# Six token groups of a linear-attention and mixer kernel, run as three pairs with seven products for eight in both channel layers

## Chip, cores and metric

One core of a Trainium2 chip. The time is that of the device, in microseconds (us), for one launch. The engines are TensorE (PE, with its weight loads as PEld), VectorE (DVE), ScalarE (ACT), GpSimd (POOL) and SyncE (SP, which here only issues DMA transfers). Transfers are issued from SP's queue and from ACT's.

## What is computed

```python
# q, k, v: batch 8, heads 8, seq 576, head_dim 64
q_s = softmax(q, axis=-1); k_s = softmax(k, axis=2)
kv = np.einsum('bhsd,bhse->bhde', k_s, v)
attn = np.einsum('bhsd,bhde->bhse', q_s, kv)
x = attn.transpose(0, 2, 1, 3).reshape(8, 576, 512)
h = np.maximum(x.transpose(0, 2, 1) @ w_tok1, 0) @ w_tok2      # 576 -> 256 -> 576
u = x + h.transpose(0, 2, 1)
out = u + np.maximum(u @ w_ch1, 0) @ w_ch2                     # 512 -> 1536 -> 512
```

## The kernel before

A product in full precision is made of three matmuls: each operand is split into a high part (ACT, a cast) and a low part (DVE, the difference), and high x high, low x high and high x low are added up in PSUM. `split` does this; its two lines, L134 and L135, serve all operands.

**Units.** A unit is one batch and two heads (32 in all, four a batch). `load_unit` loads k twice (`kt_t` and `k_t`) and q on SP's queue, `softmax_k` and `softmax_q` run on DVE, ACT and POOL, `stage_qT` turns q on DVE and through DRAM (a store `q<-cv_s` and four loads `q_t<-q`), `stage_kv`, `stage_y`, `stage_h1` and the two halves of `stage_u` run on PE. The result, u, is split and kept in one of three slots of SBUF (`slots`, `uT`), each for one group.

**Groups.** The 8 x 576 tokens are nine groups of 512. For a group, `ch1` makes a 128-row block f of the hidden layer (12 blocks), `ch2` adds its share into four PSUM banks, `out_end` adds u and stores. The list `steps` puts groups 0 and 1 first, while weights are still loaded, then group 2, and so on. `n0` is the step at which group 2 begins; `put(at, ...)` hangs the stages of the units on these steps.

**Seven products for eight.** Two by two blocks of a matrix product can be had with seven block products (P1 to P7) in place of eight, if sums of weight blocks and sums of data blocks are formed first. `keep_blocks` and `keep_sums` form the weights of ch1 and store them in DRAM (`scratch_w`), `keep_out` and `keep_out_sums` those of ch2 (`scratch_v`). From there each product's weights, 256 KB, are loaded into a ring of buffers (`ring`, L588), eight ahead, each load behind the product that used the buffer before.

Groups 3 to 6 use this for ch1 alone, each group by itself, with its two halves of 256 tokens as columns (`data_sums`, `product` at L645, `pair_a`, `pair_b`); ch2 stays at eight products for eight (`ch2`, L694). Groups 7 and 8, called GA and GB, run as a pair in `both_groups`: the two groups are the column blocks, so that a product has 512 columns, and both ch1 and ch2 take seven products (`six`, L768 and L882). Hidden blocks are put together on DVE and ACT from seven results, in banks that are handed out in turn (`bank`).

The order on each engine is made when the kernel is built, by a scheduler that goes by the order of the code and by its own estimate of times; it moves instructions past each other where nothing forbids it.

## Time and profile before

| | |
|---|---|
| median of 3 runs | 795.43 us (793.12 to 795.67) |
| profiled execution | 796.62 us, span 794.8 us, mean granted clock 0.998 |
| PE, DVE, ACT, POOL busy | 97%, 78%, 43%, 23% of the span |
| matmuls | 4824 |
| moved by DMA | 174.83 MB, mean 220 GB/s |
| groups 3 to 6 | about 331 to 670 us |
| groups 7 and 8 as a pair | about 670 us to the end |

The span runs from the first to the last instruction on the core. Busy time of an engine is the union of its instructions' durations; that of PE includes the drain of each matmul, so that a PE busy all the time may still be fed slowly. The DMA share is the mean busy share of the 16 DMA engines and can pass 1 in a short window.

### The profile page before, as it was taken

To read this page: it belongs to the slowest core of one execution; us is meant where nothing else is said; L and a number is where in the kernel's file an instruction comes from. 1 tells how busy PE (TensorE), PEld (TensorE's weight loads), DVE (VectorE), ACT (ScalarE), POOL (GpSimd) and SP (SyncE) were. 2 spreads that over 40 slices of the span, in tenths; PEclk is the share of its full clock that TensorE was granted. 3 is DMA by queue.
4 is the path that set the end of the run, shared out by engine and by line. 5 is a ranking of instruction groups with operands and counts; after the bars stand their busy time and mean duration, and the time that the engine had idled before them with its cause. 6 is when DMAs were issued, how large, how long until landed. Compare 5 with 4: busy or idle time off the path is not lost.

```text
span 794.8 us, 13455 instructions
## 1 busy us (share of the span) xinstructions
PE 769.0 (97%) x4824; PEld 670.9 (84%) x4824; DVE 618.1 (78%) x1101; ACT 341.9 (43%) x744; POOL 180.7 (23%) x130
## 2 busy tenths in 40 slices
PE   3899999999999999999999999999999999999998
PEld 2688888877888888899999999989999998888886
DVE  7979998978788874878688657888987557667971
ACT  4666433444454443434353334434444324346610
POOL 0000000011111352122211111232422320536640
PEclk9999999999999999999999999999999999999999
DMA  9655644158879785587879777999978543667776
GB/s 304 187 174 166 224 150 171 44 171 278 273 243 336 232 286 177 144 282 210 238 213 287 226 219 216 288 339 314 316 233 270 161 134 115 195 189 198 192 207 196
DMA packets 151459, 174.83 MB, mean 220 GB/s; under 512 B 51297, under 2 KB 98017, under 8 KB 151393
## 3 DMA queue, kind: packets, MB, share of 16 engines
q1 hardware_dynamic: 145056, 161.65, 67.2%
q10 hardware_dynamic: 6336, 12.32, 4.1%
q8 instruction: 38, 0.62, 0.3%
q14 instruction: 29, 0.23, 0.1%
HBM read 131.47 MB, written 42.47 MB: 219 GB/s over the span
## 4 chain that ended last, share of the span: by engine, by line
PE 70%; DVE 11%; issue 7%; DMA 7%; ACT 2%; POOL 1%; SPq 1%; DVEq 0%; POOLq 0%; ACTq 0%
PE ps_o L694 20%; PE ps_h L645 14%; PE ps_h L768 7%; PE ps_o L768 7%; PE ps_h L464 6%; PE ps_h L422 4%; PE ps_h L487 4%; PE ps_h L357 2%; DMA q_t<-in_q 2%; DMA stg<-whole 1%; PE ps_h L430 1%; PE ps_o L464 1%; PE ps_o L882 1%; DMA w<-stg 1%; DVE q_t L340 1%
## 5 line engine op out<-in xcount | busy, mean ns | idle before, releaser
L694 PE MATMUL ps_o<-h,c2h 128*128 128x512 f32 x544 | 184.2, 398 | 2.9 <-ACT h L490 1.9
L694 PEld LDWEIGHTS ps_o<-h,c2h 128*128 128x128 f32 x544 | 101.4, 188 | 23.8 <-ACT h L490 3.0
L694 PE MATMUL ps_o<-h,c2l 128*128 128x512 f32 x272 | 106.0, 393 | 0.0
L318 POOL TENSOR_TENSOR k_t<-k_t,dg 128x640 f32<-128x640 f32 x24 | 41.6, 1735 | 217.6 <-ACT dg L317 182.1
L135 POOL TENSOR_TENSOR ql<-q_t,qh 128x640 fp32r<-128x640 f32 x24 | 38.4, 1599 | 182.3 <-PE ps_o L694 104.2
L645 PE MATMUL ps_h<-th,ring 128*128 128x256 f32 x384 | 72.3, 283 | 0.0
L645 PEld LDWEIGHTS ps_h<-th,ring 128*128 128x128 f32 x384 | 60.1, 191 | 0.0
L694 PEld LDWEIGHTS ps_o<-h,c2l 128*128 128x128 f32 x272 | 51.3, 188 | 8.6
L487 PE MATMUL ps_h<-uh,c1l 128*128 128x512 f32 x144 | 56.2, 390 | 0.0
L487 PE MATMUL ps_h<-ul,c1h 128*128 128x512 f32 x144 | 56.2, 390 | 0.0
L487 PE MATMUL ps_h<-uh,c1h 128*128 128x512 f32 x144 | 56.1, 392 | 0.0
L645 PE MATMUL ps_h<-uh,ring 128*128 128x256 f32 x288 | 54.4, 282 | 0.6 <-DVE c L672 0.6
L645 PE MATMUL ps_h<-tl,ring 128*128 128x256 f32 x192 | 54.3, 283 | 0.0
L645 PEld LDWEIGHTS ps_h<-uh,ring 128*128 128x128 f32 x288 | 46.5, 190 | 2.8 <-DVE c L672 0.8
L471 ACT CAST uh<-ps_h 128x320 fp32r<-128x320 f32 (+4 forms) x76 | 24.4, 334 | 52.1 <-PE ps_h L464 32.1
L336 ACT ACTIVATE q_t<-q_t 128x640 f32<-128x640 f32 x32 | 23.6, 738 | 46.1 <-DVE q_t L327 43.1
L326 DVE TENSOR_REDUCE st<-q_t 128x10 f32<-128x640 f32 x32 | 26.1, 815 | 22.2 <-DMA q_t<-in_q 22.2
L490 ACT ACTIVATE h<-ps_h 128x512 fp32r<-128x512 f32 x36 | 21.5, 598 | 49.5 <-PE ps_h L487 42.0
L645 PE MATMUL ps_h<-ul,ring 128*128 128x256 f32 x144 | 40.6, 282 | 0.0
L645 PEld LDWEIGHTS ps_h<-tl,ring 128*128 128x128 f32 x192 | 36.8, 192 | 0.0
L472 DVE TENSOR_TENSOR ul<-ps_h,uh 128x320 fp32r<-128x320 f32 (+4 forms) x76 | 27.4, 370 | 9.0 <-ACT uh L471 8.8
L135 DVE TENSOR_TENSOR qtl<-q_t,qth 128x512 fp32r<-128x512 f32 (+1 forms) x48 | 25.6, 566 | 8.1 <-ACT qth L134 7.3
(319 smaller groups left out, 2070.2 us busy)
## 6 DMA issues: line engine op xcount, KB each, us to landing
ring<-w SPq DMA_DIRECT2D x210, 256.0 KB, 3.7
ring<-v SPq DMA_DIRECT2D x42, 256.0 KB, 3.0
kt_t<-in_kt SPq DMA_DIRECT2D x32, 320.0 KB, 3.7
q_t<-in_q SPq DMA_DIRECT2D x32, 320.0 KB, 3.7
v_t<-in_v SPq DMA_DIRECT2D x32, 320.0 KB, 4.5
stg_w<-in_w SPq DMA_DIRECT2D x18, 512.0 KB, 6.0
k_t<-in_k SPq DMA_DIRECT2D x24, 320.0 KB, 4.9
q<-cv_s SPq DMA_DIRECT2D x24, 320.0 KB, 3.2
```

Of the source, the lines that this page charges most:

```text
L135: lo_eng.tensor_tensor(lo, src, f32(hi), op=ALU.subtract)
L318: nc.gpsimd.tensor_tensor(kx, kx, dg.unsqueeze(1).broadcast_to([P, C1, P]), op=ALU.subtract)
L326: nc.vector.tensor_reduce(st[:, 0, :], qt, axis=AX.X, op=ALU.max)
L336: nc.scalar.activation(qc, qc, AF.Exp)
L422: nc.tensor.matmul(y[:, 0:TOK], a, w, start=(i == 0), stop=(i == len(mm) - 1))
L464: nc.tensor.matmul(t[:, 0:N], a, w, start=(i == 0), stop=(i == len(mm) - 1))
L471: nc.scalar.copy(uh, src).ins,
L472: nc.vector.tensor_tensor(ul, src, f32(uh), op=ALU.subtract).ins,
L487: nc.tensor.matmul(t, a[:, n, :], w, start=(i == 0), stop=(i == 3 * NJ - 1))
L645: nc.tensor.matmul(t[:, cols], a, b[:, n], start=(i == 0), stop=(i == 5))
L694: m = nc.tensor.matmul(o, a[:, cs], w, start=(first and i == 0), stop=(last and i == 2))
L768: nc.tensor.matmul(o, a, b, start=first and i == 0 and (n == 0 or not one), stop=last and i == 2 and (n == 1 or not one))
```

## The change

Groups 3 to 8 become three pairs (`NR` = 3), each run by `both_groups(r, laters[r])`, with ch1 and ch2 at seven products for eight and 512 columns throughout. `data_sums`, `product`, `pair_a`, `pair_b` and `wide_*` go.

- ch1 of a pair works in six fixed PSUM banks (`places`), and units have two others (`pu`). Products are chained in a bank: P1 is written, copied by ACT; P6 is added to it and copied; P7 is added and copied; P4 is added, and the result goes through the Relu. P5 and P3 share a second bank, P2 has a third. So the sums that DVE formed of single results are now in part sums that PE accumulates.
- The pieces of u of groups 5 to 8 are no longer split at once. `stage_u` copies them (ACT) and stores them to DRAM (`u_kept`); `make_first`, `make_second` and `make_third` load them during ch2 of the pair before, form the sums and split them. The rows to be added at the end are loaded again (`residuals`).
- Units move forward: batches 3 and 4 run beside group 2 (eight units, four before), batches 5 and 6 beside the first pair, batch 7 beside the second (`SPACE`); none is left for the third.
- The sums of the c2 weights (`keep_out_sums`) take the weights from DRAM, where `load_pair` and `load_ch` now store them (`whole_out`, ACT's queue), instead of adding high and low part on POOL; all six run beside the first pair (`SUMS_AT`).
- The weights ring has eight buffers for all of 3 x 84 products, and each product issues the load for the eighth after it.

```diff
-    KEEP = (5.5, 7.5, 37, 38.5, 40, 41.5)
-    AHEAD = 12
+    AHEAD = 9
+    SUMS_AT = (4, 9, 14, 19, 24, 29)
+    RES_AT = 31
+    SPACE = ((5, 7, 1, 8), (7, 8, 1, 10), (8, 8, 0, 0))
...
+        t = load_weights(AT_C2 + f)
+        split(*c2_row(f), t, nc.vector)
...
+        nc.scalar.dma_start(whole_out[f // 2][:, f % 2 * CW : (f % 2 + 1) * CW], t.bitcast(F32))
...
-    uT = [slots[i] for i in (0, 1, 2, 1, 0, 2, 1, 0, 2)]
+    uT = [slots[i] for i in (0, 1, 2, 1, 0)]
...
+                if g >= len(uT):
...
+                    nc.scalar.copy(x[:, k1 - k0 : k1 - k0 + a1 - a0], t[:, a0 - n0 : a1 - n0])
+                    u["kept"][g][1] = k1 + a1 - a0
+                    if a1 == S or (g == b and a1 == edge):
+                        nc.scalar.dma_start(u_kept[g][j, :, k0 : k1 + a1 - a0], x[:, 0 : k1 - k0 + a1 - a0])
+                    continue
...
-        nc.gpsimd.tensor_tensor(a, f32(wh[:, i : i + 2]), f32(wl[:, i : i + 2]), op=ALU.add)
+        nc.sync.dma_start(f32(hi), whole_out[p])
...
+    TURN = (P1, P5, P6, P2, P7, P3, P4)
+    items = [("a", 0, e) for e in TURN[:5]]
+    for p in range(1, NP):
+        items += [("a", p, P1), ("a", p, P5), ("a", p - 1, P4), ("a", p - 1, P3), ("a", p, P6), ("a", p, P2), ("a", p, P7)]
+    tail = [("b", c, e) for e in TURN for c in range(NP)]
+    items += tail[:2] + [("a", NP - 1, P4), ("a", NP - 1, P3)] + tail[2:]
...
+        for k in range(2):
+            b11, b12, b21, b22 = (h_of[2 + i][:, 1] if k else row_place() for i in range(4))
+            for t, (i, n) in ((b11, (0, k)), (b12, (1, k)), (b22, (1, 2 + k)), (b21, (0, 2 + k))):
+                nc.sync.dma_start(t, u_kept[g + i][n])
+            t0, t1 = sum_place(), sum_place()
+            split(*of_first[k], b11, nc.vector)
+            vec(t0, b12, b11, op=sub)
+            split(*of_T[0][k], t0, nc.vector)
...
+            x, y = sets[(p + r) % 2]
+            z = places[4 + p % 2]
+            o = {P1: x, P6: x, P7: x, P4: x, P5: y, P3: y, P2: z}[e]
...
+            six(w, *zip(*src), [o], e in (P1, P5, P2), e in (P4, P3, P2))
...
+            if e == P1:
+                nc.scalar.copy(c11, o)
+            elif e == P6:
+                nc.scalar.copy(c12, o)
+            elif e == P2:
+                vec(c11, o, c11, op=add)
+                relu(c11)
+            elif e == P7:
+                nc.scalar.copy(c21, o)
+                vec(c22, y, c21, op=add)
+                relu(c22)
+            elif e == P4:
+                nc.scalar.activation(c21, o, AF.Relu)
+            elif e == P3:
+                vec(c12, o, c12, op=add)
+                relu(c12)
...
+        for i, (kind, p, e) in enumerate(items):
+            for fn in later.pop(i, []):
+                fn()
+            if i == RES_AT:
+                residuals()
+            (group_product if kind == "a" else out_product)(p, e)
+            at_product[0] += 1
+            load_product()
...
-    steps += [(g, f) for g in range(2, GA) for f in range(NF)]
+    steps += [(g, f) for g in range(2, G_S) for f in range(NF)]
...
+        elif b < 5:
+            at = [n0 + 1 + 1.25 * (n - 3 * NJ) + x for x in (0, 0, 0.5, 1, 1.5)]
...
-            at = [n0 - 1 + (b - 3) * NF + 3 * j + x for x in (0, 0.5, 1, 1.5, 2)]
+            break
```

In the names of the new kernel, `b_` followed by a number is one of the six fixed banks, `pu` a unit's bank, `ring_` a weights buffer, `hb_` the hidden blocks of a pair, `w_` and `v_` the stored weights of ch1 and ch2. `uh`, `ul`, `c2h`, `c2l` and `h_` are places in SBUF that hold high and low parts of a pair's operands.

PE first. Before, in group 3: the products of a block in 256 columns, then ch2 with 512 (`h_129` a hidden block, `c2h`, `c2l` its weights, both kept in SBUF):

```order
L645 MATMUL ps_h<-th,ring_3106 128x256 x2
L645 MATMUL ps_h<-tl,ring_3106 128x256
L645 MATMUL ps_h<-th,ring_3106 128x256 x2
L645 MATMUL ps_h<-tl,ring_3106 128x256
L694 MATMUL ps_o<-h_129,c2h_1258 128x512
...
L694 MATMUL ps_o<-h_129,c2l_1259 128x512
L430 MATMUL ps_h<-kvf_98,ys 128x128 x2
```

The same place in the first pair, in the middle of ch1 (`h_135` is the operand of P4, `L372` and `L331` belong to a unit):

```order
L766 MATMUL b_3803<-ul_128,ring_3377 128x512
L766 MATMUL b_3803<-uh_127,ring_3377 128x512 x2
L766 MATMUL b_3803<-ul_128,ring_3377 128x512
L766 MATMUL b_3807<-h_135,ring_3375 128x512 x6
L372 MATMUL pu<-v_t,k_t 64x65 x10
L331 MATMUL pu<-dg,ones 128x128
L766 MATMUL b_3808<-uh_123,ring_3376 128x512 x2
L766 MATMUL b_3808<-ul_124,ring_3376 128x512
L766 MATMUL b_3808<-uh_123,ring_3376 128x512 x2
```

Each product now has 512 columns and goes to one of the fixed banks, P4 is added into a bank that holds earlier products, and no ch2 stands between; ch2's products come behind those of ch1, with their weights from the ring too.

The SP queue. Before, towards the end of group 5: a sum for ch2 is two stores `v_<-stg`, with weights of ch1 (`w_`) and transfers of a unit around it:

```order
L550 DMA v_5469<-stg 128x4x256
L173 DMA kt_t<-in_kt 128x640
L588 DMA ring_3337<-w_2321 128x512
L588 DMA ring_3103<-w_2321 128x512
L397 DMA q_6086<-cv_s 128x4x160
L550 DMA v_5469<-stg 128x4x256
L588 DMA ring_3104<-w_2478 128x512
L399 DMA q_t<-q_5820 32x4x160 x4
L588 DMA ring_3105<-w_2478 128x512
L588 DMA ring_3106<-w_2478 128x512
```

The first pair, where the sum of a block of c2 is the load of `stg` and the two stores:

```order
L641 DMA ring_3376<-w_2341 128x512
L588 DMA v_3160<-stg 128x4x256
L641 DMA ring_3371<-w_2411 128x512
L588 DMA v_3160<-stg 128x4x256
L641 DMA ring_3375<-w_2341 128x512
L181 DMA kt_t<-in_kt 128x640
L641 DMA ring_3377<-w_2411 128x512
L414 DMA q_t<-q_4226 32x4x160
L641 DMA ring_3370<-w_2411 128x512
L580 DMA stg<-out_1067 128x1024
L414 DMA q_t<-q_4226 32x4x160 x3
L641 DMA ring_3373<-w_2670 128x512
```

The stores stand as they did, but one weight set from the next, and a load of 0.5 MB more; each weight set here is one product of 512 columns.

DVE. Before, in the pair of groups 7 and 8, seven sums make a block of hidden rows (`hb`) out of banks and one split an operand (`x0l`):

```order
L838 TENSOR_TENSOR hb_7385<-ps_o,hb_7385 128x512
L840 TENSOR_TENSOR hb_7385<-ps_h,hb_7385 128x512
L844 TENSOR_TENSOR hb_7385<-ps_h,hb_7385 128x512
L842 TENSOR_TENSOR hb_7385<-ps_o,hb_7385 128x512
L850 TENSOR_TENSOR hb_7385<-ps_h,hb_7385 128x512
L847 TENSOR_TENSOR hb_7385<-ps_h,hb_7385 128x512
L135 TENSOR_TENSOR x0l<-hb_7385,x0h 128x512
L853 TENSOR_TENSOR hb_7385<-ps_o,hb_7385 128x512
```

In the first pair, with a unit (`q_t`, `rs`) and the sum of a weight block (`stg`) between:

```order
L819 TENSOR_TENSOR hb_3793<-b_3804,hb_3793 128x512
L143 TENSOR_TENSOR qtl<-q_t,qth 128x512
L143 TENSOR_TENSOR qtl<-q_t,qth 128x64
L824 TENSOR_TENSOR hb_3792<-b_3808,hb_3792 128x512
L377 TENSOR_SCALAR rs<-pu 128x1
L378 RECIPROCAL rs<-rs 128x1
L815 TENSOR_TENSOR hb_3793<-b_3805,hb_3793 128x512
L582 TENSOR_TENSOR stg<-stg 128x256
```

Three sums a block are left (L815, L819, L824), and DVE has units and weight sums to do between them, which it had not in the pair before.

## The prediction

> **What bounds the kernel now.** I read the busy table first, then windows by stage, then the chain of waits for the rate at which each kind of matmul is issued, then the waits of TensorE and of the SP queue, and last the DMA windows.

> ```profile
> PE 769.0 (97%) x4824; PEld 670.9 (84%) x4824; DVE 618.1 (78%) x1101; ACT 341.9 (43%) x744; POOL 180.7 (23%) x130
> 331.00:416.00 85.00, 85.00 (x633) 78.55 (x632) 63.80 (x118) 35.16 (x86) 16.85 (x11) 1.00 0.78 238
> 416.00:501.00 85.00, 85.00 (x623) 78.11 (x622) 64.42 (x122) 34.20 (x83) 16.74 (x11) 1.00 0.79 235
> 501.00:586.00 85.00, 83.80 (x611) 76.52 (x611) 76.08 (x141) 36.58 (x88) 26.93 (x15) 1.00 0.98 308
> 586.00:670.00 84.00, 84.00 (x603) 77.42 (x602) 54.99 (x106) 31.53 (x78) 19.48 (x13) 1.00 0.62 185
> 670.00:730.00 60.00, 60.00 (x266) 49.66 (x265) 39.25 (x59) 26.14 (x45) 26.17 (x21) 1.00 0.64 180
> ```

> The four windows from 331 to 670 hold groups 3 to 6, one each, and the last row belongs to the pair of groups 7 and 8. The columns are the window, its length, busy time of PE, weight load, DVE, ACT and POOL, then clock, DMA share and GB/s. PE is never idle except for 1.2 us in the third window. A busy PE can still be badly fed, so I check the rate of issue:

> ```profile
> 331.91 2.87 PE ps_h L645 x24
> 676.10 5.44 PE ps_o L694 x24
> 693.33 5.44 PE ps_o L768 x24
> L645 PE MATMUL ps_h<-th,ring 128*128 128x256 f32 x384 | 72.3, 283 | 0.0
> L645 PE MATMUL ps_h<-uh,ring 128*128 128x256 f32 x288 | 54.4, 282 | 0.6 <-DVE c L672 0.6
> L645 PE MATMUL ps_h<-tl,ring 128*128 128x256 f32 x192 | 54.3, 283 | 0.0
> L645 PE MATMUL ps_h<-ul,ring 128*128 128x256 f32 x144 | 40.6, 282 | 0.0
> ```

> A matmul of 256 columns takes 2.87/24 = 0.1196 us in a stream, one of 512 takes 5.44/24 = 0.2267 us, in ch2 and in the pair alike. Group 3 to 6 needs, each, 252 x 0.1196 + 144 x 0.2267 = 62.8 us; the four windows give 339/4 = 84.8 us a group, so its four units take the other 22.0 us, 5.5 us a unit. PE is the bound there, and fewer or better filled matmuls shorten the kernel one for one as long as nothing else runs out.

> **What the change removes on PE.** L645 has 384 + 288 + 192 + 144 = 1008 matmuls of 256 columns, 120.5 us. The first two pairs do the same products with 2 x 252 of 512 columns, 114.2 us: -6.3 us. In ch2 groups 3 to 6 had 4 x 144 = 576 of 512 columns, 130.6 us; two pairs need 504, 114.2 us: -16.3 us. Units are as many as before and cancel. PE work: -22.6 us.

> The 1.2 us at 525 to 535 also leave that place, since the sums of the c2 weights that were stored there go elsewhere:

> ```profile
> 525.00:530.00 5.00, 4.38 (x31) 3.88 (x30) 4.82 (x6) 1.92 (x5) 1.57 (x1) 1.00 1.08 360
> 530.00:535.00 5.00, 4.41 (x33) 3.89 (x32) 4.38 (x5) 1.59 (x5) 2.76 (x1) 1.00 1.06 359
> ```

> **What it moves: the first pair becomes crowded.** By the rates above group 2 takes 288 x 0.2267 + 8 units x 5.5 = 109 us of PE time, the first pair 504 x 0.2267 + 8 x 5.5 = 158 us, the second 114 + 4 x 5.5 = 136 us, the third 114 us. So the third pair has no units at all, and the first carries eight of them, six sums of c2 weights and the weights of 84 products. The bytes:

> ```profile
> ring<-w SPq DMA_DIRECT2D x210, 256.0 KB, 3.7
> kt_t<-in_kt SPq DMA_DIRECT2D x32, 320.0 KB, 3.7
> q_t<-in_q SPq DMA_DIRECT2D x32, 320.0 KB, 3.7
> v_t<-in_v SPq DMA_DIRECT2D x32, 320.0 KB, 4.5
> k_t<-in_k SPq DMA_DIRECT2D x24, 320.0 KB, 4.9
> q<-cv_s SPq DMA_DIRECT2D x24, 320.0 KB, 3.2
> q_t<-q SPq DMA_DIRECT2D x96, 80.0 KB, 4.1
> v<-stg SPq DMA_DIRECT2D x12, 512.0 KB, 5.0
> 240.00:270.00 30.00, 30.00 (x172) 25.41 (x172) 26.54 (x47) 13.48 (x30) 7.84 (x6) 1.00 1.04 342
> 510.00:540.00 30.00, 28.80 (x208) 26.25 (x207) 25.65 (x47) 12.33 (x29) 8.40 (x4) 1.00 1.00 319
> 540.00:570.00 30.00, 30.00 (x230) 27.52 (x230) 26.40 (x47) 14.13 (x33) 10.90 (x6) 1.00 1.01 320
> ```

> A weight set is 0.262 MB: 84 are 22 MB. A unit moves six times 0.328 MB (kt, q, k, v, the turned q out and back in four pieces), and now 0.29 MB of its result out: 2.26 MB, eight are 18 MB. A sum now reads 0.52 MB and writes 2 x 0.52: six are 9.4 MB. With results and rows of the next pair, some 6 MB, it is 55 MB in 158 us: 350 GB/s. The stage is uneven. Counted along the instructions as built, the SP queue has to bring 35.9 MB, and ACT's queue some 2.9 MB, before PE's 111th us of work of this pair: 38.8 MB, 350 GB/s over this stretch too, and less after it. At 342 GB/s (30 us without a PE stall) this takes 113 us, +2.5; at 308 GB/s (the fullest 85 us) 126 us, +15. I take 330 GB/s, between these and the two rows at 320, rather above them because there the queue was not asked for more: 117.5 us, **+6 us**, ends 0 and +15.

> [...]

> **The rest of the sum, one by one.** DVE in the first pair: 247 instructions stand between the two pair starts, at 76.08/141 = 0.54 us of the fullest window 133 us of 158, hence 0. Operands split beside POOL run slower:

> ```profile
> L135 DVE TENSOR_TENSOR ul<-hb,uh 128x512 fp32r<-128x512 f32 x13 | 12.3, 963 | 3.0 <-ACT uh L134 3.0
> 706.22 0.68 DVE L135 TENSOR_TENSOR x2l<-hb,x2h 128x512 fp32r<-128x512 f32 x1
> L836 ACT COPY hb<-ps_o 128x512 f32<-128x512 f32 x4 | 2.3, 582 | 0.0
> ```

> If all 42 take 0.96 instead of 0.68 us, DVE has 145 of 158 us, 92%; it was at 76.08/85 = 90% in the third window with PE losing 1.2 us. ACT: 274 instructions at 36.58/88 = 0.42 us, 114 of 158 us. Both stay below PE; if they run late, they delay through the SP queue (below).

> Chained banks: P6 is added into the bank of P1 and P7 into that of P6, so PE may not write again before ACT's copy (0.58 us). The order leaves at least one product, 6 x 0.2267 = 1.36 us, between P6 and P7, and more between the others: 0. If ACT is late by a copy each time, 18 x 0.3 = +5.

> Group 2 with eight units in place of four: DVE 157 instructions x 0.52 (54.99/106) = 82 of 109 us, and some 25 MB. The nearest price is what PE waited for units and drains after the start:

> ```profile
> PE ps_o L694 <- ACT h L490: 1.9, 3, 1.0
> PE ps_o L430 <- ACT ys L424: 1.9, 1, 1.9
> 120.00:180.00 60.00, 58.22 (x280) 47.23 (x278) 52.21 (x83) 24.88 (x44) 4.98 (x3) 1.00 0.40 127
> 148.89 2.04 DMA whole<-cv_s
> ```

> One such wait more, **+1** (0 to +4, one for each unit that is added). The second pair asks for 37 MB in 136 us, 272 GB/s, below all three full rows: **+1** (0 to +3). Before group 2 each load of c2 weights now also writes 0.5 MB back from its buffer; the chain already goes through such a write (2.04 us) in a window where PE lost 1.8 us and DMA was at 0.40: **+0.5** (0 to +3). At the change of banks ACT's first copies of the pair stand behind the stores of group 2's results, which wait for DVE; five products, 6.8 us, cover that: **+0.5** (0 to +4).

> On the SP queue the weights now stand behind stores that wait for DVE and ACT and behind reads of 0.5 MB; what that can cost is the third rival.

> Sum: -22.6 - 1.2 + 6 + 1 + 1 + 0.5 + 0.5 = -14.8 us. The profiled execution took 796.62 us (span 794.8, 1.8 around it), so 781.8; the median of the runs, 795.43, is 1.2 below, so **781 us**.

> **Rivals.**

> *DMA is no bound at all.* The queue takes 350 GB/s as it took 360 for 10 us, all added terms vanish: 795.4 - 23.8 = 772 us, with one small term left up to 776. For it speaks that PE lost nothing at 342 GB/s; against it, that this must last four times as long.

> *DMA at the rate of its fullest 85 us.* Then the +6 is +15 and the second pair loses its 3: 781 + 9 + 2 = 792 us, still hardly faster. The row at 308 GB/s speaks for it, the rows of 30 us against.

> *Slower: the SP queue starves the weights.* SP works in order, and a load of a unit or a store of a sum that waits for DVE holds every weight set behind it.

> ```profile
> SPq L173 <- DVE mc L299: 38.6, 12, 20.0
> SPq L588 <- PE ps_o L768: 36.8, 37, 1.9
> ```

> The queue has waited 20.0 us for DVE once; in the pair it waited only for PE to free a weight buffer. Eight buffers of 1.36 us cover 10.9 us; a wait of 20 would cost 9.1 us. From the third on the gain of 23.8 us is gone, with four of the eight units so hit it is 795.4 - 23.8 + 36.4 = 808 us. For it: DVE at 85 to 92% and kt with one buffer. Against it: the 20.0 lies among the early loads; from 331 to 670, with a unit every 21 us (every 16 us in the first pair), that wait did not reach 3 us:

> ```profile
> SPq L173 <- DVE mc L299: 4.5, 4, 2.7
> ```

> That the change would not do what it says is no rival: the instructions as built hold 432 matmuls of 512 columns more and 1008 of 256 fewer.

> **How the numbers follow.** A difference under 0.3% (2.4 us) cannot be told from none here. Forecast, 776 to 787 us: 0.45. No DMA bound, 771 to 776: 0.25. Full DMA, 787 to 795: 0.17, of which 0.07 lie within 0.3% of before. Starved weights, above 795: 0.13, of which 0.02 within. So faster 0.80, same 0.09, slower 0.11. The range 771 to 795 leaves out 0.13 above and little below; the forecast's own range is 776 to 787.

> **What would show it.** Right: L645 gone, the pair's lines at 0.2267 us a matmul; DMA above 320 GB/s for most of the first pair with PE stalls of 5 to 8 us in all there, waiting for `ring`; the third pair without stall in some 114 us. Wrong: PE full in the first pair (first rival), PE idle there by over 15 us, with SP waiting for DVE (third), or PE waiting for ACT's copies at P7, which I priced at nothing.

## The result and the profile after

The changed kernel takes 823.71 us (median of four runs, 822.18 to 824.15) against 795.54 us (793.12 to 795.67): a ratio of 1.0358, 95% interval 1.0334 to 1.0382. It is 3.6% slower where 1.8% faster was forecast, and 28.7 us above the upper end of the range. The profiled execution has a span of 821.7 us. Of all executions of this document one, of e14, was in a slow state (1529 us); it is left out, and with it the only profile of e14.

The busy table of the changed kernel, and windows by stage: first three of the kernel before (group 2; groups 3 to 6; groups 7 and 8), then four of the changed one (group 2 and the three pairs, cut at the first matmul of each). The columns are those of the prediction.

```profile
PE 763.9 (93%) x4248; PEld 635.9 (77%) x4248; DVE 633.6 (77%) x1008; ACT 411.5 (50%) x862; POOL 244.4 (30%) x173
```

```profile
242.60:331.60 89.00, 88.79 (x521) 75.03 (x520) 67.30 (x119) 39.10 (x85) 27.77 (x17) 1.00 0.74 232
331.60:670.00 338.40, 337.19 (x2459) 310.01 (x2458) 258.92 (x482) 136.87 (x330) 80.00 (x49) 1.00 0.79 242
670.00:791.00 121.00, 121.00 (x535) 100.04 (x533) 80.08 (x110) 45.29 (x78) 52.32 (x36) 1.00 0.68 192
```

```profile
241.20:372.80 131.60, 121.66 (x802) 103.86 (x800) 98.23 (x170) 58.97 (x141) 49.16 (x33) 0.99 0.76 233
372.80:553.50 180.70, 167.09 (x970) 138.92 (x968) 156.74 (x239) 106.36 (x235) 71.37 (x46) 0.98 0.94 299
553.50:703.00 149.50, 141.02 (x699) 115.44 (x700) 101.23 (x136) 76.56 (x152) 59.19 (x39) 0.98 0.72 223
703.00:818.30 115.30, 114.88 (x505) 94.21 (x503) 64.60 (x77) 48.16 (x83) 45.86 (x30) 1.00 0.70 211
```

To see what a stage loses I take its length less its matmuls at the rate of an undisturbed stream, start to start: 0.2267 us for 512 columns, 0.148 for 320, 0.1196 for 256, 0.09 for 128, 0.037 for 65 (a unit comes to about 5.4 us). By that the kernel before lost 2.2 us in group 2, 7.2 in groups 3 to 6, nothing in the last pair: 9 us. The changed one lost 17.7, 23.3, 16.4 and 0.8: 58 us. The matmuls themselves fell from 539.3 to 518.9 us, though the window of group 2 now holds 8.6 units in place of 8. So TensorE's work did shrink as predicted, and 49 us of new waiting ate it: 49.1 - 20.4 = 28.7, less 1.8 at the start and the tail, is the 26.9 between the spans. In the first three stages TensorE stood idle for 32 of the 57 us lost; in the others it counts as busy, but is fed slowly or runs at a lower clock (0.5, last section).

Where TensorE waited, by the view of waits of the changed kernel (what waited, for whom, us in total, times, longest):

```profile
PE pu L445 <- ACT ys L439: 7.5, 3, 5.0
...
PE ps_h L445 <- ACT ys L439: 3.6, 2, 2.0
...
PE pu L437 <- ACT dg L332: 3.1, 1, 3.1
PE b L766 <- DMA ring<-w: 2.8, 2, 2.4
PE pu L487 <- DVE hl L453: 2.8, 2, 1.8
PE b L766 <- DMA ring<-v: 2.1, 1, 2.1
...
PE b L766 <- ACT hb L811: 1.2, 2, 0.9
```

The largest rows are a unit's: its second product (L445) waits for ACT's copy `ys` of the first. The longest such wait, in the first pair, by the timeline (start, duration, engine, line; in brackets the idle time before and who ended it), first TensorE, then ACT, DVE and POOL:

```profile
477.73 1.23 PE L445 MATMUL pu<-kvf,ys 128*128 128x128 f32 x4 [4.96 <-ACT ys L439]
...
475.17 0.63 ACT L382 ACTIVATE kvf<-pu,rs 64x64 f32<-64x64 f32 x2 [4.34 <-DVE rs L378]
475.84 0.30 ACT L142 CAST kvh<-kvf 128x128 fp32r<-128x128 f32 x1
476.04 0.61 ACT L142 CAST uh<-sum 128x512 fp32r<-128x512 f32 x1
476.56 0.72 ACT L142 CAST qh<-q_t 128x640 fp32r<-128x640 f32 x1
477.30 0.37 ACT L439 COPY ys<-pu 128x256 f32<-128x256 f32 x1
...
470.50 1.56 DVE L143 TENSOR_TENSOR stg<-stg 128x1024 fp32r<-128x1024 f32 x1
471.98 0.14 DVE L377 TENSOR_SCALAR rs<-pu 128x1 f32<-128x1 f32 x1
472.05 1.69 DVE L143 TENSOR_TENSOR c2l<-hb,c2h 128x512 fp32r<-128x512 f32 x1
473.66 0.81 DVE L341 TENSOR_REDUCE st<-q_t 128x10 f32<-128x640 f32 x1
474.39 0.67 DVE L143 TENSOR_TENSOR ul<-hb,uh 128x512 fp32r<-128x512 f32 x1
474.99 0.15 DVE L378 RECIPROCAL rs<-rs 128x1 f32<-128x1 f32 x1
...
470.94 2.25 POOL L792 TENSOR_TENSOR sum<-hb 128x512 f32<-128x512 f32 x1
```

Read it from the end. `ys` needs only the product on TensorE, which was done by 469. But ACT started it only at 477.30: in its order three casts (1.46 us) and `kvf` stand ahead of it, and `kvf` needs `rs`, a reciprocal of 0.15 us on DVE; and on DVE the planned order puts a split, a reduction and another split ahead of that. The first split takes 1.69 us in place of 0.67, while POOL adds; two splits further ahead on DVE, at 466.05 and 467.76, took 1.79 and 2.05 us. DVE had no pause between, so I estimate that the longer splits make up some 3.5 of the 5 us (1.69 + 1.79 + 2.05 - 3 x 0.67), and the order the rest. No engine is at its limit over the stage (DVE 87%, ACT 59%); three engines in order pass one delay on. In another place the length of such a delay is plain (DVE, then POOL, same timeline):

```profile
309.57 1.53 DVE L353 TENSOR_SCALAR st<-st 128x10 f32<-128x10 f32 x1
...
309.31 1.78 POOL L333 TENSOR_TENSOR k_t<-k_t,dg 128x640 f32<-128x640 f32 x1 [11.90 <-ACT dg L332]
```

An instruction on ten columns, 0.17 us elsewhere (the median), lasts until 311.10; POOL's subtraction ends at 311.09. That the one held up the other is my reading; by what means, these two rows do not show.

### The profile page after: what moved, and what is told of

The parts are those of the page before. It is cut to its first block, busy times and chain, and to the rows that moved or that the text cites. A ratio compares the mean times of both kernels' runs of the same rounds, so it can differ in the third digit from the quotient of the medians.

```text
span 821.7 us, 12515 instructions
## 1 busy us (share of the span) xinstructions
PE 763.9 (93%) x4248; PEld 635.9 (77%) x4248; DVE 633.6 (77%) x1008; ACT 411.5 (50%) x862; POOL 244.4 (30%) x173
## 4 chain that ended last, share of the span: by engine, by line
PE 47%; DVE 22%; DMA 13%; issue 7%; ACT 4%; POOL 4%; SPq 2%; ACTq 0%; DVEq 0%; POOLq 0%
PE b L766 26%; PE ps_h L519 6%; PE ps_o L722 4%; DMA q_t<-in_q 3%; DVE ul L143 2%; PE ps_h L487 2%; DMA stg<-whole 2%; PE pu L487 2%; DVE st L352 2%; DMA stg<-out 2%; DVE q_t L342 1%; DVE qtl L143 1%; PE ps_o L487 1%; DMA out<-cv_s 1%; DMA ring<-w 1%
## 5 line engine op out<-in xcount | busy, mean ns | idle before, releaser
L766 PE MATMUL b<-uh,ring 128*128 128x512 f32 x720 | 225.0, 395 | 7.0 <-DMA ring<-w 2.8
L766 PEld LDWEIGHTS b<-uh,ring 128*128 128x128 f32 x720 | 132.8, 189 | 36.1 <-DVE h L143 2.8
L766 PE MATMUL b<-ul,ring 128*128 128x512 f32 x360 | 140.3, 394 | 1.6 <-DVE ul L143 1.5
L722 PE MATMUL ps_o<-h,c2h 128*128 128x512 f32 x288 | 95.6, 398 | 3.7 <-ACT h L522 1.9
L333 POOL TENSOR_TENSOR k_t<-k_t,dg 128x640 f32<-128x640 f32 x24 | 40.9, 1703 | 180.9 <-ACT dg L332 172.9
L766 PEld LDWEIGHTS b<-ul,ring 128*128 128x128 f32 x360 | 67.6, 189 | 17.5 <-DVE ul L143 3.3
L792 POOL TENSOR_TENSOR sum<-hb 128x512 f32<-128x512 f32 x36 | 58.5, 1632 | 67.3 <-DVE ul L143 31.4
L143 DVE TENSOR_TENSOR ul<-hb,uh 128x512 fp32r<-128x512 f32 x62 | 63.3, 1041 | 8.3 <-ACT uh L142 5.7
L722 PEld LDWEIGHTS ps_o<-h,c2h 128*128 128x128 f32 x288 | 53.3, 188 | 15.5 <-ACT h L522 2.6
L766 PE MATMUL b<-c2h,ring 128*128 128x512 f32 x168 | 53.6, 401 | 2.1 <-DMA ring<-v 2.1
L722 PE MATMUL ps_o<-h,c2l 128*128 128x512 f32 x144 | 55.6, 391 | 0.0
## 6 DMA issues: line engine op xcount, KB each, us to landing
ring<-w SPq DMA_DIRECT2D x126, 256.0 KB, 4.2
ring<-v SPq DMA_DIRECT2D x126, 256.0 KB, 3.5
stg_w<-in_w SPq DMA_DIRECT2D x18, 512.0 KB, 6.4
```

Of the source, the lines that this page charges most:

```text
L143: lo_eng.tensor_tensor(lo, src, f32(hi), op=ALU.subtract)
L333: nc.gpsimd.tensor_tensor(kx, kx, dg.unsqueeze(1).broadcast_to([P, C1, P]), op=ALU.subtract)
L722: m = nc.tensor.matmul(o, a[:, cs], w, start=(first and i == 0), stop=(last and i == 2))
L766: nc.tensor.matmul(outs[0 if one else n], a, b, start=first and i == 0 and (n == 0 or not one), stop=last and i == 2 and (n == 1 or not on ...
L792: pl(t, h[:, 3], h[:, 0], op=sub)
```

## The experiments

Four theories were tested: A, DVE is late because its instructions take longer while POOL's run (1.69 us for 0.67 above), and ACT and TensorE wait in order behind it. B, the serial chain of a unit (its q goes through DRAM and two buffers) cannot turn round as fast as units now come. C, DMA bandwidth. D, units or stages stand too close, or the engines' order is at fault. Stage lengths in us, with the loss in parentheses; one run where no interval is given. (The expectations of e1 to e4 cut the changed kernel's stages in another way, at 131, 177, 147 and 120 us. The stages of e12 are those of its profiled execution, which took 784.0 us.)

| kernel | whole | group 2 | first pair | second | third |
|---|---|---|---|---|---|
| changed | 823.7 | 131.6 (17.7) | 180.7 (23.3) | 149.5 (16.4) | 115.3 (0.8) |
| e1 no units in pairs | 752.0 | 132.7 (21.8) | 137.4 (22.9) | 117.6 (3.1) | 116.9 (2.4) |
| e7 and no c2 sums | 740.2 | 134.9 (24.0) | 120.6 (6.3) | 121.2 (6.5) | 116.8 (2.3) |
| e4 no c2 sums | 835.9 | 136.0 (22.3) | 181.7 (25.8) | 153.0 (18.2) | 116.3 (1.8) |
| e3 no turn of q | 824.3 | 129.8 (15.9) | 176.5 (23.9) | 154.9 (16.9) | 119.0 (4.5) |
| e2 no operand sums | 804.2 | 133.2 (19.3) | 165.4 (10.5) | 138.5 (2.8) | 116.1 (1.6) |
| e9 sums only write | 802.8 | 131.8 (18.1) | 170.6 (12.3) | 139.0 (6.3) | 114.4 (0) |
| e8 sums on DVE | 823.3 | 133.6 (19.7) | 171.5 (16.6) | 153.6 (17.6) | 115.6 (1.1) |
| e5 no POOL in units | 802.7 | 123.5 (9.8) | 180.9 (25.0) | 140.0 (5.2) | 116.4 (1.9) |
| e16 it only writes there | 800.8 | 128.6 (14.7) | 174.0 (17.7) | 138.9 (4.7) | 115.7 (1.2) |
| e6 neither on POOL | 791.1 | 125.6 (11.7) | 166.2 (11.0) | 136.9 (1.5) | 117.7 (3.2) |
| e17 all of it only writes | 798.2 | 125.5 (11.8) | 177.3 (16.1) | 137.0 (7.3) | 114.6 (0.1) |
| e10 no shift of q | 820.6 | 133.6 (19.9) | 185.0 (26.7) | 140.9 (8.6) | 115.9 (1.4) |
| e13 group 2 spread | 830.2 | 125.8 (16.4) | 181.4 (24.0) | 153.5 (18.5) | 116.1 (1.6) |
| e12 light units | 789.6 | 125.3 (13.2) | 167.1 (13.4) | 136.7 (1.7) | 118.5 (4.0) |
| e11 and sums on DVE | 784.9 | 127.7 (15.6) | 163.0 (9.6) | 136.6 (1.6) | 119.9 (5.4) |
| e15 and spread | 779.2 | 117.8 (8.1) | 164.1 (10.8) | 136.4 (1.2) | 119.3 (4.8) |

Every edit also makes the scheduler plan another order. Group 2, which e1, e2, e4, e7 and e8 do not touch, took 131.6 to 136.0 us: differences of 4 us in one stage mean nothing.

**e1, the pairs without units.**

```diff
-    for r, (b0, b1, x0, dx) in enumerate(SPACE):
+    for r, (b0, b1, x0, dx) in enumerate(()):
```

> Leaves out the twelve units of batches 5 to 7, so the three pairs hold nothing but their own products, weight sets and sums of c2 weights; results of the left out units are replaced by any rows of q. The pairs took 177, 147 and 120 us; their products alone are 504 x 0.2267 = 114.3 us each, and the units' matmuls 65 us in all. If the units cause the loss, by the length of their own chain or by the load they put on DVE, each pair comes to 114 to 118 us and the whole to about 725 us. If the pair loses by itself (chained banks, ACT's copies, POOL's sums beside DVE's splits, weight sets), the first pair stays at 125 or more and the whole is 740 to 757 us. Group 2 is not touched and stays at about 131 us under every theory.

Pairs two and three lose 2 to 3 us, with all of POOL's sums: the pair's own machinery costs little. The first is as the second expectation has it, and loses 22.9 without any unit. There SP stands before the first sum of c2 weights (one row of its waits):

```profile
SPq L580 <- DMA out<-stg: 24.4, 1, 24.4
```

**e7, and without the sums of c2 weights** (their products load weights of ch1).

```diff
-        laters[0].setdefault(x, []).append(lambda p=p: keep_out_sums(p))
+        pass
```

> Leaves out the late units of batches 5 to 7 as before, and the six sums of c2 weights too. With the units left out alone the first pair took 137.4 us for 114.5 us of matmuls, where SP stood 24.4 us before the first sum's load, for a buffer whose result was still being stored. If the sums and the queue behind them are that loss, the first pair comes to 115 to 120 us and the whole to 728 to 736 us (752.0 with them). If it is POOL beside DVE or the start of the pair, it stays at 130 or more and the whole at 745 or more.

The first pair comes to 120.6: in a pair without units the sums cost 16.6 us. The whole fell less than expected (740.2 in place of 728 to 736).

**e4, without these sums, units in place.**

> Leaves out the six sums of c2 weights in the first pair (9.4 MB, 24 additions and 6 splits on DVE, some 18 us of it, 6 copies on ACT); the products that would read them load weights of ch1 instead. Theory C (DMA bandwidth in the first pair): 177 falls to 150 to 160 us, nothing else changes, the whole 800 to 808 us. Theory A (DVE late in the first pair): DVE is relieved of 18 us of 154, the pair falls by about 8 to 15 us to 162 to 169, the whole 809 to 816. Theory B (unit chain): under 4 us.

9.4 MB fewer, and DVE busy for 127 us in place of 157, and yet the pair is no shorter: neither C's 150 to 160 nor A's 162 to 169 came. But one new wait stands out, first SP's, then TensorE's for the weights behind it:

```profile
SPq L836 <- DMA out<-part: 6.8, 2, 6.3
```

```profile
PE b L766 <- DMA ring<-w: 8.0, 2, 6.9
```

A row of results is loaded into a buffer whose old content is still being stored, and the queue waits with all weights behind it. That is the prediction's third rival, though with another cause, in a plan that the changed kernel does not have. Its 8 us are about what A had forecast as a gain, so this run decides against neither A nor C, and what the sums cost in the changed kernel itself it does not show.

**e3, q not through DRAM.**

```diff
-        nc.sync.dma_start(dq.rearrange("y p f -> p y f"), turned.rearrange("p y c t -> p y (c t)"))
...
-        back = qx.rearrange("p c t -> p (c t)").rearrange("p (x c t) -> p c x t", x=P // Q, t=Q)
+        back = turned.rearrange("p y c t -> p c y t")
```

> Leaves out the way of q through DRAM in the late units (one store and four loads, 0.66 MB a unit and some 7 us of its chain); the split reads the transposed blocks directly, DVE and ACT do as many instructions as before. Theory B (the unit's serial chain): group 2 falls from 131 to 112 to 117 us, the first pair from 177 to 160 to 165, the whole to about 785 us. [...] Theory C (DMA bandwidth): 5.2 MB less in group 2 and in the first pair each, at 300 GB/s up to 17 us where DMA is full, which is the first pair only: 177 to 160 there, group 2 as it is, 805 us.

824.3 us, with group 2 at 129.8 in place of B's 112 to 117: as far as the turn through DRAM goes, B falls, which I had held for the likeliest from the chain of waits, where q's loads and stores stand in every round. C falls with it (176.5 in the first pair, 160 forecast).

**e2, operand sums left out, and e9, sums that only write** (the lines of e2, then of e9, where the write stands three times for each sum; P1's two sums likewise).

```diff
-                pl(t, h[:, 3], h[:, 0], op=sub)
-                if e == P4:
-                    pl(t, h[:, 2], t, op=sub)
+                t = h[:, 3]
...
+                nc.gpsimd.memset(t, 0.5)
```

> Leaves out the sums of ch2's moving operands on POOL (30 subtractions in each pair); the blocks themselves are used as operands, DVE's and ACT's instructions stay as they are. [...] Theory B (the serial chain of a unit through q's buffers and its turn through DRAM): no change beyond 4 us. Theory C (DMA bandwidth): no change beyond 4 us.

> Each of POOL's 30 sums of operands in a pair becomes three writes of a constant to the same tile: POOL is as long at it (a write of 128x128 took 0.207 us) and stands in the same place of the chain, but reads nothing; the sums themselves are left out. [...] If the cost is that POOL answers late (1.4 to 1.6 us a sum), the pairs stay at 177 or more and 146 or more, the whole at 818 or more.

e2 gives 19.5 us, within A's 795 to 810: the first two pairs are 26 us shorter, both within their ranges (160 to 168 and 135 to 140), and 6 are lost ahead of group 2 and in it. It alone does not tell POOL's time from its reads; e9 does. The splits' group of DVE and a write's group of POOL, first the changed kernel, then e2 (where 18 more operands go by this name), then e9 (us in total, mean ns):

```profile
L143 DVE TENSOR_TENSOR ul<-hb,uh 128x512 fp32r<-128x512 f32 x62 | 63.3, 1041 | 8.3 <-ACT uh L142 5.7
```

```profile
L143 DVE TENSOR_TENSOR ul<-hb,uh 128x512 fp32r<-128x512 f32 x80 | 56.9, 724 | 19.2 <-ACT uh L142 18.0 <-PE b L766 1.1
```

```profile
L143 DVE TENSOR_TENSOR ul<-hb,uh 128x512 fp32r<-128x512 f32 x62 | 46.0, 746 | 14.1 <-ACT uh L142 10.5 <-PE b L766 3.4
...
L794 POOL MEMSET sum<- 128x512 f32 x36 | 18.9, 526 | 0.7
```

Three writes are 1.58 us, as long as the sum was, and POOL was busy 74.8 us in the first pair (71.4 before). Yet the splits are at 746 ns and the whole at 802.8, where A had 803 to 811. So POOL's busy time alone does not make the splits long; with the sums, which read, they took 1041 ns on average. One thing besides the reads is gone in e9, though: a write does not wait for the operands of the sum, so that the tiles are ready earlier. In the changed kernel ACT waited for POOL's sums for 2.5 us in the first pair, too little for the 10 us that e9 gains there, but for 13.1 us in the second (5.2 in e9); there the two are not told apart.

**e8, the sums on DVE.**

> Moves the 30 sums of operands in each pair from POOL to DVE; nothing is left out. DVE gets 30 x 0.68 = 20 us more in each pair, POOL 45 us less. [...] If it is DVE's amount of work that makes it late, the first pair grows to 182 or more, the second stays at 145 or more, the whole at 818 or more.

823.3 us, no gain. The first pair gains 9 us, the second loses 4: the splits are at 705 ns, but DVE's unit work now stands behind 20 us of sums. In the second pair POOL was busy for only 10 us and the splits took 0.69 us, and it still lost 17.6: long splits are not the only way to be late there. A's forecast of 802 to 811 was wrong here. Nor need long splits cost anything by themselves: in the third pair of the changed kernel, which has no units, they are at their longest (DVE's lines from 703 to 818.3), and the stage loses 0.8 us.

```profile
L143 DVE TENSOR_TENSOR ul<-hb,uh 128x512 fp32r<-128x512 f32 x19 | 22.7, 1224 | 5.6 <-ACT uh L142 3.7 <-PE b L766 1.7
```

**e5, e16: the units' two instructions on POOL, left out or only writing; e6, e17: these and the sums.** The added lines are those of e5 and e6, then of e16 and e17, three writes each, to `ql` too.

```diff
-        nc.gpsimd.tensor_tensor(kx, kx, dg.unsqueeze(1).broadcast_to([P, C1, P]), op=ALU.subtract)
...
-        split(qh, ql, qc, nc.gpsimd)
+        ql = qh
+        nc.scalar.copy(qh, qc)
...
+        nc.gpsimd.memset(kx, 0.5)
```

> Leaves out POOL's two instructions in each late unit (the subtraction of k's maxima and the low part of q; the high part is used twice). Measured before: group 2 took 131.6 us (113.9 by matmuls), the pairs 180.7, 149.5 and 115.3. [...] Theory D (the stages of a unit stand so close on PE that DVE and ACT cannot answer in time, with or without POOL): group 2 stays at 127 or more, the first pair at 176 or more, the whole at 812 or more.

> POOL's two instructions in each late unit become three writes of a constant each to the same tiles, of 128x640, some 2 us for 1.7 us before, so that POOL is busy as long but reads nothing; the subtraction of k's maxima and the low part of q are left out. With the instructions left out the whole took 802.7 us, group 2 123.5 and the second pair 140.0. If POOL's reads were the cost, it is the same here: the whole 798 to 808 us, group 2 121 to 127, the second pair 138 to 143. If it was POOL's time in the unit's chain, group 2 stays at 129 or more, the second pair at 146 or more, the whole at 815 or more.

> Leaves out POOL's two instructions of each late unit and the 30 sums of operands in each pair, so that from group 2 on POOL only adds rows of results. Without the operand sums alone the stages took 133.2, 165.4, 138.5 and 116.1 us and the whole 804.2. Theory A: group 2 116 to 122, the first pair 157 to 161 (its matmuls alone are 155 to 157), the second 134 to 137, the whole 782 to 790 us, faster than the kernel before. Theory D: group 2 at 127 or more, the pairs at 164 and 138, the whole 798 to 804 us.

> Both together: the units' instructions and the pairs' sums on POOL only write, and POOL is as busy as before or busier. With all of them left out the whole took 791.1 us. [...]

e5 gives 21 us: 8 in group 2, 9.5 in the second pair, and 4.5 by which group 2 begins earlier. Group 2 stays above A's 116 to 122, and the first pair does not gain at all, as D has it. e16 gives as much in all (800.8) with POOL as busy as before (52 us in group 2, 49 before), so that the reads count again, or the wait for the operands, which falls away here too. But its stages share the gain otherwise: group 2, at 128.6, misses its range, and the first pair gains 6.7. Which stage gains from the units' two instructions is thus not settled, but for the second pair. e6 is at 791.1, 1 above A's range, with group 2 and the first pair 4 to 5 us above theirs; D's ranges fail too. In it TensorE keeps its pace through the first pair's fullest DMA windows:

```profile
390.00:400.00 10.00, 10.00 (x55) 8.64 (x55) 7.33 (x12) 6.69 (x13) 0.00 (x0) 1.00 1.09 361
520.00:530.00 10.00, 10.00 (x47) 7.70 (x46) 7.37 (x14) 3.88 (x7) 0.00 (x0) 1.00 1.02 381
```

e17, at 798.2, misses the range for POOL's reads as the whole of its cost (786 to 796) by 2. Its first pair (177.3) is 8 above the forecast of 163 to 169, and POOL was busy there for 85 us, 14 more than in the changed kernel: POOL's time may count for something too, but one run does not show it. The loss over all four stages falls from 58.2 to 27.4 without POOL's instructions (e6) and to 35.3 without their reads and waits for operands (e17): that is 31 and 23 of the 49 us.

**e10, less work for DVE alone** (no maxima of q, no subtraction).

```diff
-        st, _ = shifted.pop(u["n"]) if u["n"] in shifted else shift_q(qc)
+        if u["early"]:
+            st, _ = shifted.pop(u["n"]) if u["n"] in shifted else shift_q(qc)
+        else:
+            st = sm.tile([P, 3, G], F32, name="st")
```

> Leaves out, in the late units, the search for q's maxima and their subtraction: two instructions of DVE, 0.81 and 0.82 us, of each unit, and two steps of its chain (the shift cancels in the quotient). [...]

820.6 us, where 800 to 810 was forecast if DVE's amount of work counts as much as POOL's instructions, and 815 or more if those alone decide: 1.63 us of DVE less in each unit gains nothing in group 2 or the first pair, 9 us in the second. Less work on DVE alone does not help in the stages that lost most.

**e12, e11: light units.** Both softmaxes of late units without the shift by the maximum (it cancels; inputs here are far from overflow), q's low part on DVE, 24 sums a pair on POOL (e12) or on DVE (e11).

```diff
-        split(qh, ql, qc, nc.gpsimd)
+        split(qh, ql, qc, nc.vector)
...
-                t = sum_place()
-                pl(t, h[:, 3], h[:, 0], op=sub)
+                t = h[:, 0]
+                if e == P6:
+                    vec(t, h[:, 3], t, op=sub)
...
```

> The same light units, with the 24 sums of operands in each pair on POOL. Group 2 as with the sums on DVE, 117 to 122 us. [...]

> Relieves POOL and DVE together. Late units take no maxima of k and q (the shift cancels in both quotients; on these inputs no exponential comes near its limit), so k's transposed load, two small matmuls, two copies on ACT, two reductions and one subtraction on DVE and one on POOL fall away for each; q's low part goes to DVE; the operands' sums go to DVE and are 24 in place of 30 a pair, since one of them is kept. POOL is left with the rows of results. By the stages seen so far: group 2 117 to 122 us, the first pair 160 to 168, the second 134 to 140, the third 115 to 117, the whole 770 to 785 us, faster than the kernel before. If what is left of the loss is the order in which the engines' instructions stand, group 2 stays at 124 or more and the first pair at 170 or more, the whole at 788 or more.

789.6 (ratio to before 0.9918, interval 0.9891 to 0.9944) and 784.9 (0.9877, 0.9838 to 0.9916). With POOL off the units, sums on DVE no longer hurt; the difference between the two is within their intervals. So e12's forecast of 8 to 14 us for the sums on POOL was too high: its first pair (167.1, 170 to 176 forecast) and second (136.7) are shorter than expected, with POOL reading for 36 us in the second. Against e5, where POOL is off the units and keeps the sums as well, the first pair loses 13.4 in place of 25.0 (with 24 sums for 30): the units' own work and chain count there too.

**e13, e15: group 2's units earlier and further apart, alone and with e11.**

```diff
-            at = [n0 + 1 + 1.25 * (n - 3 * NJ) + x for x in (0, 0, 0.5, 1, 1.5)]
+            at = [n0 - 1 + 1.43 * (n - 3 * NJ) + x for x in (0, 0.5, 1, 1.5, 2)]
```

> The changed kernel with the eight units of batches 3 and 4 begun two steps earlier and 1.43 steps apart in place of 1.25, their stages half a step apart each, as in the kernel before; nothing else. If the density of the units is what is left of group 2's loss, group 2 and what stands ahead of it end earlier: the first pair begins at 362 to 367 us in place of 372.8, the whole 812 to 818 us in place of 823.7. If not, the first pair begins at 371 or later and the whole stays at 820 or more.

> The changed kernel with light units and the operands' sums on DVE, with the units of batches 3 and 4 spread as in the first run of this call. If the density in group 2 costs what is left there (13 to 15 us), the first pair begins some 6 to 10 us earlier than 359.3 and the whole is 775 to 779 us. If not, it stays at 783 to 787.

In the changed kernel it only moves the loss: group 2 begins at 248.2 in place of 241.2, the first pair at 374.0 in place of 372.8, and 830.2 is worse. With light units the first pair begins at 353.0 in place of 359.3, and the whole is 779.2 us, 0.9833 of before (0.9788 to 0.9878): faster than both kernels. Its stages:

```profile
235.20:353.00 117.80, 113.72 (x750) 98.25 (x748) 79.19 (x151) 56.46 (x123) 22.47 (x16) 1.00 0.78 244
353.00:517.10 164.10, 159.95 (x918) 135.63 (x919) 125.13 (x241) 100.44 (x212) 2.48 (x2) 0.98 0.97 308
517.10:653.50 136.40, 136.40 (x729) 114.95 (x728) 92.84 (x161) 75.36 (x149) 0.00 (x0) 1.00 0.78 241
653.50:772.80 119.30, 116.59 (x505) 95.38 (x503) 62.76 (x101) 49.29 (x84) 0.00 (x0) 0.99 0.69 209
```

**e14, the kernel before with light units.**

> The kernel before the change with the light units (no maxima of k and q in the late units, q's low part on DVE). There TensorE lost next to nothing, so only the two small matmuls of each of 24 units fall away, 0.25 us a unit: 795.1 - 6 = 789 us, 787 to 791, and the changed kernel with light units (784.9) is still 4 us faster. If DVE and POOL held that kernel up as well, it falls to 780 to 785 and nothing is left of the advantage of the pairs.

783.7 us (0.9875, 0.9836 to 0.9914), 5 us better than forecast and as the second expectation has it: against e11 (784.9) nothing is left of the pairs' advantage. What the light units relieve in this kernel no profile shows. So of e15's gain most is the lighter units'; the pairs with the spread units add 4.5 us, and the two intervals overlap.

## Why the prediction was wrong

- TensorE's work: -22.6 forecast. Measured -20.4 in the windows, -23.7 with the 0.6 unit that came over from the stage ahead of group 2. Right; the new pair runs 0.2267 us a matmul, and the third pair, forecast at 114 us without a stall, took 115.3.
- **The step that failed: "DVE in the first pair: ... hence 0" and "Both stay below PE; if they run late, they delay through the SP queue".** I compared an engine's busy share with the stage's length. DVE had 87% there, about as expected (though of a longer stage: 156.7 us busy, in place of 133 to 145), and was late all the same: what TensorE needs is a 0.15 us instruction of a unit that stands behind splits, and beside POOL instructions of 1.3 to 2.3 us three of those took 1.69 to 2.05 us in place of 0.67. I saw the 963 ns row and turned it into 12 us more of DVE time. The delay went through ACT's order, not through SP. The timeline shows the path; e2 and e9 show, with 15 and 10 us in the first pair, that POOL's sums are part of the cause. The pair for which DVE was put at 0 and DMA at +6 lost 23.3 us.
- In the kernel before the same things were there, apart: units with little on POOL (80 us in 338) in groups 3 to 6, sums on POOL in a pair without units. e1's second and third pairs show the same: sums without units cost 2 to 3 us. The change put both in one place.
- Group 2, +1 for "one such wait more": lost 17.7 us, 15.5 more than before. The rows behind it were no price for this stage: the 1.9 us at L430 is a wait at 28 us, among the early units, and two of the three waits at L694 (0.96 and 0.76 us) lie in the stretch from 120 to 180, with 5 us of POOL in 60; group 2 now has 49 in 132. e5 takes back 8, e16 only 3; e15 shows that with light units the spacing counts for 7.5.
- Second pair, +1: lost 16.4. The same step; e2, e5, e9, e16 each bring it to 3 to 6.
- First pair, +6 for DMA: lost 23.3, none of it waiting for weights. The first rival had the mechanism: e6 runs 10 us at 361 and at 381 GB/s without a stall. The 308 to 342 GB/s that I took for DMA's limit are passed there.
- The slower rival had the right sign and the wrong path: SP's waits for DVE in the first pair were at most 3.8 us. Priced at 0.5 each, the writes ahead of group 2 and the banks were right to 2 us; ACT's copies cost 1.2.
- Not settled: some 18 of the 49 us stay when POOL's instructions for units and sums are left out (e6), 26 when they only write (e17). In e5, e6, e11 and e12 group 2 stayed at 123.5 to 127.7, each time above the 116 (or 117) to 122 that were forecast. The c2 sums (e7 against e1) and the spacing in group 2 (e15 against e11) are part of it, but e4 and e13 gained nothing in the changed kernel itself.

## What to carry to other kernels

An engine at 75 to 87% is not cover: where engines work in order, as ACT does from 475.17 to 477.67 above, price the longest thing that may stand ahead of the small instruction that the bound engine waits for, and do so along every engine on the path. Before two kinds of work are put into one stage, measure what the instructions of the one take beside those of the other: here DVE's splits took 1041 ns on average with POOL's sums, 746 with writes in their place (e9). A probe that keeps an engine as busy but takes its reads away tells the cost of its instructions' reads from that of its busy time; it also takes away the wait for what was read, which has to be looked up beside it.

## What was not expected of the hardware

```profile
312.00:313.00 1.00, 0.78 (x7) 0.57 (x5) 0.97 (x2) 0.95 (x4) 0.00 (x0) 1.00 0.72 115
313.00:314.00 1.00, 0.00 (x0) 0.00 (x0) 0.88 (x3) 1.00 (x3) 0.00 (x0) 1.00 0.91 306
314.00:315.00 1.00, 0.18 (x1) 0.18 (x2) 1.00 (x2) 0.74 (x2) 0.50 (x1) 0.91 1.08 378
315.00:316.00 1.00, 1.00 (x5) 1.00 (x6) 0.90 (x2) 0.00 (x0) 1.00 (x1) 0.50 1.13 367
316.00:317.00 1.00, 1.00 (x4) 0.81 (x3) 1.00 (x2) 0.63 (x2) 0.04 (x1) 0.50 1.13 332
...
318.00:319.00 1.00, 1.00 (x5) 0.86 (x4) 0.90 (x4) 0.00 (x0) 0.00 (x0) 0.88 0.49 122
```

The wait of 4.96 us was followed by 4.3 us of work at half rate, while one of 3.14 us at 368 had no such sequel. From group 2 on the clock was at one half in four stretches, from 314.83, 475.25, 564.00 and 666.40, of 3.41 us each but for the second with 6.83 (2.5 of it still waiting): 14.6 us of work at half rate, some 7 of the 58 us lost. Their beginnings are 160.42, 88.75 and 102.40 us apart, which is 47, 26 and 30 times 3.413 us, so in this run they lie on a grid of that step. The wait of 2.04 us lies wholly in the last 3.41 us before a beginning, that of 3.14 us half on each side of a grid point (369.44). What in the step before a beginning decides is not shown: before 564.00 it held two waits of 0.69 and 0.97 us, while 1.89 us of waiting in the step before 700.54 had no sequel.
